# A bank of its own for each feature, two copies ahead of a mask, and stores and loads issued a step later

## The chip, the cores and the metric

The kernel runs on one core of one Trainium2 chip. The metric is the device time of one execution in microseconds. Its engines are TensorE (PE, with its weight loads as PEld), VectorE (DVE), ScalarE (ACT), GpSimd (POOL) and SyncE (SP), which here issues all DMAs from one queue, in order.

## What is computed

Block attention, then two expert layers without routing, all in float32. The matmuls run on pairs of float32r numbers (a high part and a low part), three products for each.

```python
x = attention(q, k, v)              # 8 x 8 heads, 576 tokens in blocks of 64, head size 64
h = x @ moe_w_in                    # 4608 x 512 @ 512 x 2048
g = maximum(h, 0) + alpha * minimum(h, 0)
x = g @ moe_w_out                   # 2048 x 512
h = x @ moe2_w_in
g = h - tanh(h)
out = g @ moe2_w_out                # 4608 x 512
```

## The kernel before

The 4608 tokens are nine blocks of 512, the 2048 hidden columns 16 features of 128. The program has two halves, and the order of its instructions on each engine is the order in which the code is written.

**First half** (`step_one`, 144 steps, one feature of one block each): an up product of 12 matmuls, a leaky ReLU, a split of its result into high and low part, and the down product of an earlier feature. When a block is done, `put_bank` (L583) copies four PSUM banks to `yst`, a tile with three buffers, and stores them to `ysc`. Beside this the attention of later blocks runs (`raw`, `rawn` and `v` are its loads), and 32 pieces of the second layer's weights are converted: `park_load` (L187) loads one as `rw`, two steps later `park_convert` (L198) makes its high part `whi` and its low part in `mr` and, at the end of that step (L224, L225), stores both to DRAM as `wu` and `wd`. `at(step, ...)` (L729) puts such calls into steps. Loads of attention inputs that belong to the next step are issued after those stores.

**Second half** (`layer_two`, L986): 72 pairs of features, q = 0 to 71, eight to each block; p = q mod 8. The up product of a pair is done by Strassen's scheme: seven products p1, p5, p6, p2, p3, p7, p4 of six matmuls each (L1011, 128x256 outputs), into two PSUM banks h0 and h1, one for each feature. Between them stand the down matmuls of earlier features (`downs`, L972, 128x512), 24 to a pair in four gaps of 5, 7, 7 and 5; pair 0 has 4, 5, 5, 0 and pair 1 has 5, 5, 7, 5. In a pair:

- p1 and p5 go into the halves of h1; ScalarE copies the first to h0 (L1045) and the second to `p5`, a part of `ptb` (L1046); p6 waits for these copies.
- after p6 and p2 VectorE adds into h0 (L1017), which p3 waits for; after p7 it adds into h1, which p4 waits for.
- then `act_g` and `tanhshrink` (L539) make g of each feature: ScalarE does sq, th, w and mask (L546 to L549), VectorE four operations and a COPY_PREDICATED that takes th where the mask says so (L550 to L554). ScalarE splits off the high part (L533) and GpSimd the low part (L536) in the next pair.

So ScalarE does eight operations (four for each feature) and then the two copies of the next pair. h0 is complete with p3, h1 with p4.

The banks alternate by pair. Even pairs have the two banks of one tile (`new_banks`, L320, pool `ps_a`, two banks in one buffer); odd pairs have two tiles of a bank each from `ps_h`. The framework derives an instruction's waits from the tiles it touches.

The down weights of layer two come through a ring of four slots (`fetch_down`, L246): each slot is refilled when its feature is done. Slots 2 and 3 are the place of the last feature of the first half; at the end of pair 0 (L1072) the kernel issues their first loads (`wd_2`, `wd_3`) and one of `wu`. Pair 1 issues the load of the next `yraw` (L612) and, as the last block of the first half is finished in its gaps, four `ysc` stores.

Of the kernel before, what the change touches and what calls it, by code (L numbers as in the profile page):

```python
# [27 lines left out]
def kernel(  # L28
# [19 lines left out]
    nc = tc.nc  # L48
# [17 lines left out]
    att = ctx.enter_context(tc.tile_pool(name="att", bufs=1))  # L66
# [2 lines left out]
    dram = ctx.enter_context(tc.tile_pool(name="dram", bufs=1, space=bass.MemoryType.DRAM))  # L69
    ps_h = ctx.enter_context(tc.tile_pool(name="ps_h", bufs=2, space=bass.MemoryType.PSUM))  # L70
    ps_y = ctx.enter_context(tc.tile_pool(name="ps_y", bufs=1, space=bass.MemoryType.PSUM))
    ps_a = ctx.enter_context(tc.tile_pool(name="ps_a", bufs=1, space=bass.MemoryType.PSUM))

    ident = const.tile([P, P], F32, name="ident")
    nalpha_sb = const.tile([P, KF], F32, name="nalpha_sb")
# [2 lines left out]
    edge_sb = const.tile([P, 1], F32, name="edge_sb")  # L78
    xar = xpool.tile([P, 2, 2, KD, NB], F32R, name="xar")
# [7 lines left out]
    wsplit = {}  # L87
# [103 lines left out]
    wu2, wd2, park_raw = {}, {}, {}  # L191
# [11 lines left out]
    def park_convert(kind, n, c):  # L203


        mr = wide.tile([P, 8, P], F32, tag="r", name="mr", bufs=1)
        flat = mr.rearrange("p s m -> p (s m)")
        to_f32_b([to_f32_a(park_raw.pop((kind, n, c)), flat[:, :512], flat.bitcast(I32)[:, 512:])])
        hi = wide.tile([P, 8, P], F32R, tag="w", name="whi")
        if kind == "d":  # L210
            m, h, lo = mr[:, 0:4], hi[:, 0:4], mr[:, 4:8]
            wd2[n] = dram.tile([P, 2, 4, P], F32, name=f"wd2_{n}")
            to = [wd2[n][:, i] for i in range(2)]
        else:
            for o, x, y, op in ((4, 1, 3, ALU.add), (1, 0, 1, ALU.subtract), (5, 4, 0, ALU.subtract),
                                (6, 2, 5, ALU.subtract)):
                nc.gpsimd.tensor_tensor(out=mr[:, o], in0=mr[:, x], in1=mr[:, y], op=op)  # L217
            m, h, lo = mr[:, 0:7], hi[:, 0:7], mr[:, 0:7]
            if n not in wu2:
                wu2[n] = dram.tile([P, 7, 2, 2, P], F32, name=f"wu2_{n}")  # L220
            to = [wu2[n][:, :, i, c] for i in range(2)]
        nc.scalar.activation(out=h, in_=m, func=AF.Copy)
        nc.gpsimd.tensor_tensor(out=lo.bitcast(F32R), in0=m, in1=h.bitcast(F32), op=ALU.subtract)
        nc.sync.dma_start(out=to[0], in_=h.bitcast(F32))  # L224
        nc.sync.dma_start(out=to[1], in_=lo)  # L225

    wu_home = {}

    def fetch_up(d):
        wu_home[d] = home(d, [P, 4, 2, 2, P], F32R, "wu")  # L230
        u = 4 * d
        while u < 4 * d + 4:
            n, o = divmod(u, 7)
            k = min(7 - o, 4 * d + 4 - u)
            nc.sync.dma_start(out=wu_home[d][:, u - 4 * d:u - 4 * d + k].bitcast(F32), in_=wu2[n][:, o:o + k])
            u += k
# [78 lines left out]
    def new_banks(name):  # L315

        return ps_a.tile([P, 2, 512], F32, tag="a", name=name)
# [192 lines left out]

    sq2 = None

    def act_g(layer, f, hp, n):
        g = gpool.tile([P, n], F32, tag="g", name="g", bufs=2)
        if layer == 1:
            tanhshrink(g, hp, n, f)
        else:
            neg = stage.tile([P, 512], F32, tag="st", name="neg")[:, :n]
            nc.scalar.activation(out=neg, in_=hp, func=AF.Relu, scale=-1.0)  # L519
            nc.scalar.activation(out=g, in_=hp, func=AF.Relu)  # L520
            nc.vector.scalar_tensor_tensor(  # L521
                out=g, in0=neg, scalar=nalpha_sb[:, f:f + 1], in1=g, op0=ALU.mult, op1=ALU.add
            )
        hi = gpool.tile([P, n], F32R, tag="ghi", name="ghi")
        lo = gpool.tile([P, n], F32R, tag="glo", name="glo")
        return g, hi, lo
# [11 lines left out]
    def tanhshrink(g, hp, n, f):  # L538


        ca, cb, ce, cc = TS
        sq = sq2[:, f % 2]
        w = att.tile([P, n], F32, tag=("p", "pt")[f % 2], name="w")
        th = vpool.tile([P, n], F32, tag="v", name="th")
        mask = ktc.rearrange("p u h c d -> p (u h c d)")[:, f % 2 * n:(f % 2 + 1) * n]
        nc.scalar.activation(out=sq, in_=hp, func=AF.Square)  # L546
        nc.scalar.activation(out=th, in_=hp, func=AF.Tanh)
        nc.scalar.activation(out=w, in_=sq, func=AF.Square, bias=bias_sb)  # L548
        nc.scalar.activation(out=mask, in_=sq, func=AF.Relu, bias=edge_sb)  # L549
        nc.vector.scalar_tensor_tensor(out=g, in0=sq, scalar=cc, in1=hp, op0=ALU.mult, op1=ALU.mult)  # L550
        nc.vector.tensor_tensor(out=th, in0=hp, in1=th, op=ALU.subtract)  # L551
        nc.vector.scalar_tensor_tensor(out=g, in0=w, scalar=ce, in1=g, op0=ALU.add, op1=ALU.mult)  # L552
        nc.vector.scalar_tensor_tensor(out=g, in0=sq, scalar=ca, in1=g, op0=ALU.add, op1=ALU.mult)  # L553
        nc.vector.copy_predicated(g, mask.bitcast(U32), th)  # L554

    def down(layer, f, g, acc, ends, cuts=((0, 4),)):
        w = wsplit[f, 1]
# [109 lines left out]
    def at(step, fn, *args, first=False):  # L667


        place = {att_s: 0, att_v: 0, att_a_natural: 0, att_a: 3, park_convert: 4, convert: 4, split_w: 4}.get(  # L670
            fn, 1 if first else 2)
        events.setdefault(step, ([], [], [], [], []))[place].append((fn, args))
# [312 lines left out]
    def downs(n):  # L985
        for _ in range(min(n, len(todo))):  # L986
            todo.pop(0)()

    def layer_two(queue, late):
# [1 line left out]

        H = NB // 2
        nonlocal sq2
        banks0, sq2 = new_banks("hps"), att.tile([P, 2, NB], F32, tag="qt", name="sq2")
        p5s = ptb.rearrange("p e h a i -> p (e h a i)").rearrange("p (u t) -> p u t", u=2)

        def leave(j):
# [3 lines left out]
        for layer, f, g, acc, j, t0, ends in queue:  # L1001
            todo.extend(down_items(layer, f, g, acc, ends, lambda f=f: wsplit[f, 1], leave(j) if f == ends[1] else None))
        split_g(*late.pop(), nc.vector)
        nc.tensor.matmul(out=banks0[:, 0], lhsT=wsplit[KF - 1, 1][:, 0, 0:P], rhs=xar[:, 0, 0, 0], start=True, stop=True)
        pairs = {0: (banks0[:, 0], banks0[:, 1])}

        def product(name, n, p, o, start=False):
            w, x = w_up(p, name), XSLOT[n, name]
# [19 lines left out]
            todo[-1] = (lambda last: lambda: (last(), release()))(todo[-1])  # L1028

        LATER = (0, 2, 4, 5, 6, 7)  # L1030
        made, accs = [], {}
        for q in range(NPAIR * n1):
            n, p = divmod(q, NPAIR)
            if q == 1:
                pairs[1] = tuple(ps_h.tile([P, NB], F32, tag="h", name="hps") for _ in range(2))
            h0, h1 = pairs[q % 2]
            p5 = p5s[:, q % 2]
            gaps = (5, 7, 7, 5) if q > 1 else (4, 5, 5, 0) if q == 0 else (5, 5, 7, 5)
            if p == 0:
                accs[n] = []  # L1040
            if p == 1 and n + 1 < n1:
                load_y(n1 + n + 1)
            product("p1", n, p, h1[:, :H], start=True)
            product("p5", n, p, h1[:, H:])
            nc.scalar.activation(out=h0[:, :H], in_=h1[:, :H], func=AF.Copy)  # L1045
            nc.scalar.activation(out=p5, in_=h1[:, H:], func=AF.Copy)  # L1046
            downs(gaps[0])
            product("p6", n, p, h1[:, :H])
            product("p2", n, p, h0[:, :H])
            add(h0[:, H:], h1[:, :H], p5)  # L1050
            for op in (x_ops(n)[9:] if p == 0 and n else x_ops(n + 1)[7:9] if p == NPAIR - 1 and n + 1 < n1 else ()):
                op()
            for m in made:
                split_hi(*m[2])
            for m in reversed(made):
                split_lo(*m[2], nc.gpsimd)
            if n + 1 < n1 and 2 <= p < NPAIR - 1:
                for op in x_ops(n + 1)[LATER[p - 2]:LATER[p - 1]]:
                    op()
            downs(gaps[1])  # L1060
            if made:
                enlist(*made[0])
            product("p3", n, p, h0[:, H:])
            product("p7", n, p, h1[:, :H])
            add(h1[:, H:], h1[:, :H], p5)
            downs(gaps[2])
            product("p4", n, p, h1[:, :H])
            downs(gaps[3])
            if made:
                enlist(*made[1])  # L1070
            made = [(n, 2 * p + e, act_g(1, 2 * p + e, hp, NB), accs[n]) for e, hp in enumerate((h0, h1))]
            if q == 0:  # L1072
                ring_slots(KF - 2)
                for i in (2, 3):
                    fetch_down(i)
                fetch_up(KF - 3)
        downs(KF)
        for m in made:
            split_g(*m[2], nc.vector)
# [41 lines left out]
```

## Time and profile before

| | us |
|---|---|
| median of 3 runs | 1771.32 (1770.65 to 1772.48) |
| the profiled execution | 1773.57 |
| its span | 1771.8 |
| TensorE busy | 1652.6 (93%) |
| VectorE busy | 1167.4 (66%) |
| ScalarE busy | 980.7 (55%) |
| GpSimd busy | 412.8 (23%) |

The span is that of the profiled execution alone, 1.8 us less than its whole time. TensorE is the busiest engine and has about half of the chain that ended last (51%); its busy time is near the span, so what can be won is the time in which it waits. The first half ends at about 890 us. All stretches, starts and waits in the rows are microseconds from the start of the span.

### The profile page before, as it was taken

Reading aid. Unit: us, or ns where it says so; the run is one execution under the profiler, and the core shown is the slowest. Engines: PE = TensorE matmul, PEld = TensorE weight load, DVE = VectorE, ACT = ScalarE, POOL = GpSimd, SP = SyncE. Lnnn points to the kernel's source line nnn. Section 1 sums busy time; section 2 is a strip of 40 time slices with the busy share of each in tenths; the row PEclk is TensorE's granted clock in tenths of the full one; section 3 lists DMA queues with packets and bytes.
Section 4 is the critical chain, followed back from the end, with each engine's and each line's share of the span. In section 5 each row is a group of like instructions: output and inputs, shape, how many; then the busy total and the mean of one; then the engine's idle time right before and its main releaser. Section 6 shows DMA issues by size and latency. Waiting matters only on the chain.

```text
span 1771.8 us, 28197 instructions
## 1 busy us (share of the span) xinstructions
PE 1652.6 (93%) x10702; PEld 1397.4 (79%) x10702; DVE 1167.4 (66%) x1829; ACT 980.7 (55%) x1796; POOL 412.8 (23%) x348
## 2 busy tenths in 40 slices
PE   7899999999998999999979898989898998989898
PEld 6688888888887888788867787877777787878777
DVE  7878756775775767654236666676666666666666
ACT  5666544554554554544336556556565656565554
POOL 1000001111121111112104334342333333333321
PEclk9999999999999999999989999999999999999999
DMA  9551524443544444426632333323242424243232
GB/s 244 166 172 34 130 63 105 113 120 105 129 104 114 104 135 96 133 63 211 214 131 94 119 97 111 117 92 132 87 141 84 143 87 132 91 132 95 90 113 83
DMA packets 259383, 209.47 MB, mean 118 GB/s; under 512 B 173216, under 2 KB 210096, under 8 KB 258224
## 3 DMA queue, kind: packets, MB, share of 16 engines
q1 hardware_dynamic: 259248, 207.68, 39.5%
q8 instruction: 84, 1.38, 0.3%
q14 instruction: 51, 0.42, 0.1%
HBM read 163.59 MB, written 44.04 MB: 117 GB/s over the span
## 4 chain that ended last, share of the span: by engine, by line
PE 51%; DVE 9%; ACT 5%; issue 4%; DMA 2%; POOL 2%; SPq 1%; DVEq 0%; POOLq 0%; ACTq 0%
PE y L972 17%; PE hps L1011 15%; PE y L563 9%; PE hps L505 9%; DVE g L550 2%; DVE g L553 2%; DVE g L552 2%; SPq L308 1%; DVE th L551 1%; DMA ysc<-yst 1%; ACT w L548 1%; ACT ktc L549 1%; ACT sq L546 1%; POOL glo L536 1%; DVE hps L1017 1%
## 5 line engine op out<-in xcount | busy, mean ns | idle before, releaser
L505 PE MATMUL hps<-xar,w 128*128 128x512 f32 (+1 forms) x1740 | 422.2, 392 | 5.9 <-ACT kt L342 5.3
L505 PEld LDWEIGHTS hps<-xar,w 128*128 128x128 f32 x1740 | 328.7, 190 | 74.9 <-ACT kt L342 5.8
L1011 PEld LDWEIGHTS hps<-xar,wu 128*128 128x128 f32 x2160 | 286.4, 191 | 84.1 <-ACT ptb L1046 53.9
L1011 PE MATMUL hps<-xar,wu 128*128 128x256 f32 x2160 | 303.6, 285 | 51.7 <-ACT ptb L1046 42.1
L972 PE MATMUL y<-wd,ghi 128*128 128x512 f32 x1152 | 321.3, 394 | 8.7 <-ACT yst L588 8.7
L533 ACT ACTIVATE ghi<-g 128x512 fp32r<-128x512 f32 x288 | 181.5, 630 | 247.9 <-DVE g L554 143.5
L563 PE MATMUL y<-ghi,w 128*128 128x512 f32 x1136 | 296.9, 394 | 6.4 <-ACT yst L588 5.0
L536 POOL TENSOR_TENSOR glo<-g,ghi 128x512 fp32r<-128x512 f32 x142 | 180.8, 1294 | 495.1 <-ACT ghi L533 252.8
L563 PEld LDWEIGHTS y<-ghi,w 128*128 128x128 f32 x1136 | 210.2, 188 | 51.8 <-ACT yst L588 5.5
L972 PEld LDWEIGHTS y<-wd,ghi 128*128 128x128 f32 x1152 | 203.9, 190 | 37.6 <-ACT yst L588 9.1
L546 ACT ACTIVATE sq<-hps 128x512 f32<-128x512 f32 x144 | 86.3, 600 | 194.9 <-PE hps L1011 188.1
L521 DVE SCALAR_TENSOR_TENSOR g<-neg,nalpha_sb,g 128x512 f32<-128x512 f32 x144 | 107.9, 749 | 122.8 <-ACT g L520 122.8
L536 DVE TENSOR_TENSOR glo<-g,ghi 128x512 fp32r<-128x512 f32 x146 | 131.3, 899 | 82.6 <-ACT ghi L533 82.1
L550 DVE SCALAR_TENSOR_TENSOR g<-sq,hps 128x512 f32<-128x512 f32 x144 | 98.2, 682 | 128.7 <-PE y L972 107.4
L972 PE MATMUL y<-wd,glo 128*128 128x512 f32 x576 | 166.1, 395 | 5.8 <-POOL glo L536 5.8
L1017 DVE TENSOR_TENSOR hps<-hps,ptb 128x256 f32<-128x256 f32 x144 | 62.5, 434 | 155.5 <-PE hps L1011 155.3
L563 PE MATMUL y<-glo,w 128*128 128x512 f32 x568 | 162.6, 390 | 0.2
L519 ACT ACTIVATE neg<-hps 128x512 f32<-128x512 f32 x144 | 85.6, 594 | 125.2 <-PE hps L505 123.3
L1011 PE MATMUL hps<-xw,wu 128*128 128x256 f32 x864 | 126.2, 285 | 23.6 <-ACT ptb L1046 20.5
L1011 PEld LDWEIGHTS hps<-xw,wu 128*128 128x128 f32 x864 | 116.3, 191 | 36.6 <-ACT ptb L1046 25.9
L217 POOL TENSOR_TENSOR mr<-mr 128x128 f32<-128x128 f32 x64 | 33.9, 540 | 473.5 <-DVE mr L138 471.0
L554 DVE COPY_PREDICATED g<-ktc,th 128x512 f32<-128x512 uint32 x144 | 123.3, 856 | 15.5 <-DVE g L553 0.5
(113 smaller groups left out, 2031.0 us busy)
## 6 DMA issues: line engine op xcount, KB each, us to landing
wd<-wd SPq DMA_DIRECT2D x144, 512.0 KB, 3.5
yraw<-ysc SPq DMA_DIRECT2D x9, 1024.0 KB, 6.1
out_dram<-yst SPq DMA_DIRECT2D x36, 256.0 KB, 2.2
raww<-in_moe_w_in_dram SPq DMA_DIRECT2D x16, 512.0 KB, 5.6
v<-in_v_dram SPq DMA_DIRECT2D x32, 256.0 KB, 3.9
raww<-in_moe_w_out_dram SPq DMA_DIRECT2D x16, 512.0 KB, 5.6
rw<-in_moe_w_in_dram SPq DMA_DIRECT2D x16, 512.0 KB, 4.7
rw<-in_moe_w_out_dram SPq DMA_DIRECT2D x16, 512.0 KB, 4.4
```

Source lines behind the costliest of these rows:

```text
L505: nc.tensor.matmul(out=hp[:, cols], lhsT=w[:, a, m], rhs=x[b][:, kk, cols], start=(kk == 0 and i == 0), stop=(kk == KD - 1 and i == 2),)
L519: nc.scalar.activation(out=neg, in_=hp, func=AF.Relu, scale=-1.0)
L521: nc.vector.scalar_tensor_tensor(out=g, in0=neg, scalar=nalpha_sb[:, f:f + 1], in1=g, op0=ALU.mult, op1=ALU.add)
L533: nc.scalar.activation(out=hi, in_=g, func=AF.Copy)
L536: lo_engine.tensor_tensor(out=lo, in0=g, in1=hi.bitcast(F32), op=ALU.subtract)
L546: nc.scalar.activation(out=sq, in_=hp, func=AF.Square)
L550: nc.vector.scalar_tensor_tensor(out=g, in0=sq, scalar=cc, in1=hp, op0=ALU.mult, op1=ALU.mult)
L554: nc.vector.copy_predicated(g, mask.bitcast(U32), th)
L563: nc.tensor.matmul(out=acc[t], lhsT=lhsT, rhs=rhs, start=(f == ends[0] and i == 0), stop=(f == ends[1] and i == 2))
L972: nc.tensor.matmul(out=acc[t], lhsT=lhsT, rhs=rhs, start=(f == ends[0] and i == 0), stop=(f == ends[1] and i == 2))
L1011: nc.tensor.matmul(out=o, lhsT=w[:, a, c], rhs=x[:, b, c], start=start and i == 0 and c == 0, stop=i == 2 and c == 1, skip_group_check=True,)
L1017: nc.vector.tensor_tensor(out=o, in0=a, in1=b, op=ALU.add)
```

## The change

1. **Banks.** `ps_a` is closed when the second half begins, and a pool `ps_b` of single banks takes its place: an even pair's h0 and h1 are two tiles (`hpb`).
2. **Mask.** `tanhshrink` returns its last two instructions, mask and COPY_PREDICATED, as a function `end`. For the first feature of a pair it is called at once, as before. For the second it is called in the next pair, behind the copies L1045 and L1046.
3. **Ring.** The first loads of slots 2 and 3 and that of `wu` are issued at the end of pair 1, not of pair 0.
4. **Stores.** `park_convert` no longer stores; `park_store` does so in the step behind it, after that step's attention loads and ahead of the next `park_load`.

```diff
-        nc.sync.dma_start(out=to[0], in_=h.bitcast(F32))
-        nc.sync.dma_start(out=to[1], in_=lo)
+        park_raw[kind, n, c] = ((to[0], h.bitcast(F32)), (to[1], lo))
+
+    def park_store(kind, n, c):
+        for to, x in park_raw.pop((kind, n, c)):
+            nc.sync.dma_start(out=to, in_=x)
...
-        nc.scalar.activation(out=mask, in_=sq, func=AF.Relu, bias=edge_sb)
+
+        def end():
+            nc.scalar.activation(out=mask, in_=sq, func=AF.Relu, bias=edge_sb)
+            nc.vector.copy_predicated(g, mask.bitcast(U32), th)
+
...
-        nc.vector.copy_predicated(g, mask.bitcast(U32), th)
+        return end
...
     for i, park in enumerate(parks):
+        if i:
+            at(2 * KF + 4 + 3 * i, park_store, *parks[i - 1])
         at(2 * KF + 4 + 3 * i, park_load, *park)
         at(2 * KF + 6 + 3 * i, park_convert, *park)
+    at(2 * KF + 4 + 3 * len(parks), park_store, *parks[-1])
...
-        banks0, sq2 = new_banks("hps"), att.tile([P, 2, NB], F32, tag="qt", name="sq2")
+        pairs_ctx.close()
+        ps_b = ctx.enter_context(tc.tile_pool(name="ps_b", bufs=2, space=bass.MemoryType.PSUM))
+        banks0 = [ps_b.tile([P, NB], F32, tag="b", name="hpb") for _ in range(2)]
+        sq2 = att.tile([P, 2, NB], F32, tag="qt", name="sq2")
...
             nc.scalar.activation(out=p5, in_=h1[:, H:], func=AF.Copy)
+            while ends:
+                ends.pop()()
             downs(gaps[0])
...
-            made = [(n, 2 * p + e, act_g(1, 2 * p + e, hp, NB), accs[n]) for e, hp in enumerate((h0, h1))]
-            if q == 0:
+            made = [(n, 2 * p + e, act_g(1, 2 * p + e, hp, NB, ends if e else None), accs[n]) for e, hp in enumerate((h0, h1))]
+            if q == 1:
                 ring_slots(KF - 2)
```

No instruction is added or taken away on TensorE, VectorE, ScalarE or GpSimd. Three places show what moves. What stands in brackets are the counters that an instruction waits for: those of engines, or of DMAs (DMAHW).

ScalarE, from the end of pair 2 (even) to the copies of pair 3; ktc is the mask. Before:

```order
L546 ACTIVATE sq_8761<-hps 128x512 [waits DVE_49,PE_49]
L547 ACTIVATE th<-hps 128x512
L548 ACTIVATE w<-sq_8761,bias_sb 128x512 [waits Activation_49]
L549 ACTIVATE ktc<-sq_8761,edge_sb 128x512
L546 ACTIVATE sq_8761<-hps 128x512 [waits DVE_49]
L547 ACTIVATE th<-hps 128x512
L548 ACTIVATE w<-sq_8761,bias_sb 128x512 [waits Activation_49]
L549 ACTIVATE ktc<-sq_8761,edge_sb 128x512
L1045 ACTIVATE hps<-hps 128x256 [waits PE_49]
L1046 ACTIVATE ptb<-hps 128x256
```

And now:

```order
L554 ACTIVATE sq_8766<-hpb 128x512 [waits PE_49]
L555 ACTIVATE th<-hpb 128x512
L556 ACTIVATE w<-sq_8766,bias_sb 128x512 [waits Activation_49]
L559 ACTIVATE ktc<-sq_8766,edge_sb 128x512
L554 ACTIVATE sq_8766<-hpb 128x512 [waits DVE_49,PE_49]
L555 ACTIVATE th<-hpb 128x512
L556 ACTIVATE w<-sq_8766,bias_sb 128x512 [waits Activation_49]
L1063 ACTIVATE hps<-hps 128x256 [waits PE_49]
L1064 ACTIVATE ptb<-hps 128x256
L559 ACTIVATE ktc<-sq_8766,edge_sb 128x512
```

The mask of the second feature went from before the two copies to behind them, and the first sq lost its wait for VectorE; the second sq has one for TensorE. In the programs the counter that the first sq waits for stands at p4's last matmul before, and at p3's last matmul now; in odd pairs it stands at p3's in both.

SP, pairs 0 to 2; wd_2 and wd_3 are the first loads of ring slots 2 and 3. Before:

```order
L235 DMA wu<-wu_7_7888 128x1536 [waits DMAHW2_49]
L250 DMA wd<-wd_2_3995 128x1024 [waits DMAHW3_49,PE_49]
L250 DMA wd<-wd_3_4142 128x1024 [waits DMAHW4_49]
L235 DMA wu<-wu_7_7888 128x2048 [waits DMAHW5_49]
L612 DMA yraw<-ysc_2616 128x4x512 [waits DMAHW6_49,Pool_49]
L589 DMA ysc_8762<-yst 128x512 [waits DMAHW7_49,Activation_49]
L589 DMA ysc_8762<-yst 128x512 [waits DMAHW0_49,Activation_49]
L589 DMA ysc_8762<-yst 128x512 [waits DMAHW1_49,Activation_49]
L589 DMA ysc_8762<-yst 128x512 [waits DMAHW2_49,Activation_49]
L250 DMA wd<-wd_4_4716 128x1024 [waits DMAHW3_49,PE_49]
```

And now:

```order
L239 DMA wu<-wu_7_7888 128x1536 [waits DMAHW2_49]
L624 DMA yraw<-ysc_2616 128x4x512 [waits DMAHW3_49,Pool_49]
L601 DMA ysc_8767<-yst 128x512 [waits DMAHW4_49,Activation_49]
L601 DMA ysc_8767<-yst 128x512 [waits DMAHW5_49,Activation_49]
L601 DMA ysc_8767<-yst 128x512 [waits DMAHW6_49,Activation_49]
L601 DMA ysc_8767<-yst 128x512 [waits DMAHW7_49,Activation_49]
L254 DMA wd<-wd_4_4716 128x1024 [waits DMAHW0_49,PE_49]
L254 DMA wd<-wd_2_3995 128x1024 [waits DMAHW1_49]
L254 DMA wd<-wd_3_4142 128x1024 [waits DMAHW2_49]
L239 DMA wu<-wu_7_7888 128x2048 [waits DMAHW3_49]
```

The load of yraw and the four stores of ysc stand ahead of wd_2 and wd_3 now; wd_4, the refill of slot 0, stands ahead of these too and waits for the end of pair 1.

SP in the first half, where one block of tokens ends (at about 530 us of the trace). Before:

```order
L106 DMA rw<-in_moe_w_out_dram 128x512
L308 DMA raw<-in_q_dram 32x8x32 x7
L224 DMA wd_6_5417<-whi 128x512
L225 DMA wd_6_5417<-mr 128x512
L308 DMA raw<-in_q_dram 32x8x32 x7
L269 DMA v<-in_v_dram 128x8x64
L106 DMA rw<-in_moe_w_out_dram 128x512
L589 DMA ysc_5474<-yst 128x512 x4
```

And now:

```order
L107 DMA rw<-in_moe_w_out_dram 128x512
L312 DMA raw<-in_q_dram 32x8x32 x14
L273 DMA v<-in_v_dram 128x8x64
L229 DMA wd_6_5417<-whi 128x512
L229 DMA wd_6_5417<-mr 128x512
L107 DMA rw<-in_moe_w_out_dram 128x512
L601 DMA ysc_5474<-yst 128x512 x4
```

The two stores of converted weights (whi and mr) stand behind 14 attention loads, not between 7 and 7.

## Rows read from the trace of the kernel before

**Rows 1.** Busy time by stretch: length, PE, PEld, DVE, ACT, POOL, granted clock, DMA

```profile
100.00:300.00 200.00, 200.00 (x1324) 163.94 (x1323) 145.55 (x227) 109.02 (x183) 5.86 (x8) 1.00 0.35 87
900.00:1000.00 100.00, 81.62 (x480) 70.58 (x479) 61.38 (x94) 55.20 (x105) 30.72 (x24) 0.95 0.34 111
1200.00:1400.00 200.00, 179.27 (x1095) 156.13 (x1094) 132.87 (x203) 120.91 (x230) 73.92 (x56) 1.00 0.36 118
```

**Rows 2.** TensorE's waits: total us, times, longest

```profile
PE hps L1011 <- ACT ptb L1046: 62.6, 36, 2.8
PE hps L1011 <- DVE hps L1017: 11.9, 9, 1.5
PE y L972 <- ACT yst L588: 8.7, 1, 8.7
PE y L972 <- POOL glo L536: 5.8, 8, 0.7
```

**Rows 3.** Timeline of pairs 26 to 28: start, length, instruction, idle before

```profile
1211.62 1.60 PE L1011 MATMUL hps<-xar,wu 128*128 128x256 f32 x12
...
1213.65 0.39 ACT L1046 ACTIVATE ptb<-hps 128x256 f32<-128x256 f32 x1
...
1214.22 1.59 PE L1011 MATMUL hps<-xar,wu 128*128 128x256 f32 x12
...
1214.54 0.77 DVE L554 COPY_PREDICATED g<-ktc,th 128x512 f32<-128x512 uint32 x1
...
1215.92 0.43 DVE L1017 TENSOR_TENSOR hps<-hps,ptb 128x256 f32<-128x256 f32 x1 [0.60 <-PE hps L1011]
...
1217.26 0.88 PE L1011 MATMUL hps<-xar,wu 128*128 128x256 f32 x6
...
1220.31 0.88 PE L1011 MATMUL hps<-xw,wu 128*128 128x256 f32 x6
...
1221.22 0.60 ACT L546 ACTIVATE sq<-hps 128x512 f32<-128x512 f32 x1 [4.14 <-PE hps L1011]
...
1222.18 1.59 PE L1011 MATMUL hps<-xar,wu 128*128 128x256 f32 x12
...
1225.30 0.72 ACT L549 ACTIVATE ktc<-sq,edge_sb 128x512 f32<-128x512 f32 x1
...
1226.65 1.70 PE L1011 MATMUL hps<-xar,wu 128*128 128x256 f32 x12 [1.71 <-ACT ptb L1046]
...
1234.72 1.48 PE L1011 MATMUL hps<-xar,wu 128*128 128x256 f32 x11
```

**Rows 4.** Timeline of pair 31, VectorE beside GpSimd

```profile
1273.81 1.57 POOL L646 TENSOR_TENSOR xar<-yraw,xar 128x512 fp32r<-128x512 f32 x1 [6.38 <-ACT xar L645]
...
1274.26 1.67 DVE L553 SCALAR_TENSOR_TENSOR g<-sq,g 128x512 f32<-128x512 f32 x1
```

**Rows 5.** Timeline of pairs 0 to 2, where the second half begins

```profile
890.62 1.60 PE L1011 MATMUL hps<-xar,wu 128*128 128x256 f32 x12
...
899.28 0.60 ACT L546 ACTIVATE sq<-hps 128x512 f32<-128x512 f32 x1 [6.24 <-PE hps L1011]
...
910.90 11.33 SPq L589 DMA_DIRECT2D ysc<-yst  x4
...
921.29 0.60 ACT L588 ACTIVATE yst<-y 128x512 f32<-128x512 f32 x1 [12.39 <-DMA ysc<-yst]
...
923.39 2.47 PE L1011 MATMUL hps<-xar,wu 128*128 128x256 f32 x12
```

**Rows 6.** Timeline: the last pair's first product

```profile
1746.10 1.60 PE L1011 MATMUL hps<-xar,wu 128*128 128x256 f32 x12
```

**Rows 7.** Timeline of the first half, one block of tokens ends

```profile
528.41 3.43 SPq L308 DMA_DIRECT2D raw<-in_q_dram  x7
...
533.05 5.91 SPq L589 DMA_DIRECT2D ysc<-yst  x4
...
538.02 0.60 ACT L588 ACTIVATE yst<-y 128x512 f32<-128x512 f32 x1 [7.40 <-DMA ysc<-yst]
```

More of the change, by code (lines that the diff above doesn't have):

```diff
@@ L71 @@
     ps_y = ctx.enter_context(tc.tile_pool(name="ps_y", bufs=1, space=bass.MemoryType.PSUM))
-    ps_a = ctx.enter_context(tc.tile_pool(name="ps_a", bufs=1, space=bass.MemoryType.PSUM))
+    pairs_ctx = ctx.enter_context(ExitStack())
+    ps_a = pairs_ctx.enter_context(tc.tile_pool(name="ps_a", bufs=1, space=bass.MemoryType.PSUM))
     ident = const.tile([P, P], F32, name="ident")
@@ L511, with act_g @@
     sq2 = None
-    def act_g(layer, f, hp, n):
+    def act_g(layer, f, hp, n, ends=None):
         g = gpool.tile([P, n], F32, tag="g", name="g", bufs=2)
         if layer == 1:
-            tanhshrink(g, hp, n, f)
+            end = tanhshrink(g, hp, n, f)
+            if ends is None:
+                end()
+            else:
+                ends.append(end)
         else:
@@ L1003, in layer_two @@
         split_g(*late.pop(), nc.vector)
-        nc.tensor.matmul(out=banks0[:, 0], lhsT=wsplit[KF - 1, 1][:, 0, 0:P], rhs=xar[:, 0, 0, 0], start=True, stop=True)
-        pairs = {0: (banks0[:, 0], banks0[:, 1])}
+        nc.tensor.matmul(out=banks0[0], lhsT=wsplit[KF - 1, 1][:, 0, 0:P], rhs=xar[:, 0, 0, 0], start=True, stop=True)
+        pairs = {0: tuple(banks0)}
         def product(name, n, p, o, start=False):
@@ L1030, in layer_two @@
         LATER = (0, 2, 4, 5, 6, 7)
-        made, accs = [], {}
+        made, accs, ends = [], {}, []
         for q in range(NPAIR * n1):
@@ L1076, in layer_two @@
                 fetch_up(KF - 3)
+        ends.pop()()
         downs(KF)
```

## The prediction

> **What bounds the kernel now.** I read the busy time by stretch first. In the first half TensorE is busy without a gap (200.00 of 200 us), at the full granted clock of 1.00, which is 2.4 GHz. In the second half it is busy 179.27 of 200 us at the same clock, and 81.62 of 100 us at a mean of 0.95 where that half begins [rows 1]. No other engine is above 133 of 200 there. So the second half is TensorE's work plus TensorE's waits, and the list of its waits says which: 62.6 us in 36 waits for ACT's copy L1046, 11.9 us for VectorE's add L1017, one wait of 8.7 us for the copy yst, 5.8 us for glo [rows 2]. The timeline then shows where the 62.6 us come from. In pair 26, an even one, p3 starts at 1217.26 and p4 at 1220.31; ScalarE has idled 4.14 us when its first sq starts at 1221.22, just as p4 ends (1220.31 + 0.88), although h0 has been complete since p3. Its eight operations and two copies then run to 1226.6, and pair 27's p6 starts at 1226.65 after a wait of 1.71 us. Behind pair 27, an odd one, there is none: in pair 26 the copy L1046 begins at 1213.65, ends at 1214.04, and p6 starts at 1214.22 with no idle time noted [rows 3]. The wait list of the first sq has TensorE's p4 in even pairs and p3 in odd ones, as the section on the change says; both features of an even pair stand in one tile.
>
> **The price of an even pair's late start.** Pair 26 takes 10.56 us from its p1 to the next (1211.62 to 1222.18) and holds no wait of TensorE. Pair 27 does the same number of matmuls in 12.54 us (1222.18 to 1234.72) [rows 3]. The loss is 1.98 us, a little more than the 1.71 us shown as idle. Pair 26 is therefore my measure of a pair without a wait, and everything above 10.56 us in the second half is the stock that the change can draw on.
>
> **Banks (part 1).** Even pairs get the waits that odd pairs have. What follows an odd pair is an even one, so a pair such as 26 is an image of what each pair becomes. Pairs 2 to 70 run from 923.39 [rows 5] to 1746.10 [rows 6], 822.71 us for 69 pairs; at 10.56 us each they are 728.6 us. The difference of 94.1 us is more than 34 late odd pairs times 1.98 us (67.3 us). The rest is what comes after the late start in the same pairs: VectorE's chain of the second feature, late by the same time, runs into GpSimd's work (pair 31: GpSimd's L646 of 1.57 us at 1273.81, and an L553 of 1.67 us beside it [rows 4], where a COPY_PREDICATED of the same 128x512 took 0.77 in pair 26 [rows 3]), and the add is late for p3, or glo for the first down product of a block; those are the 11.9 and 5.8 us [rows 2]. With the chain starting earlier these fall away too. The slack says by how much: in pair 26 VectorE idles 0.60 us before its add at 1215.92, which ends at 1216.35, 0.91 us before p3 [rows 3]; so it may be 1.5 us late for nothing. Two GpSimd operations beside the chain cost it some 0.9 us each (1.67 against 0.77), 1.8 us in a pair with two such, 0.3 us above the slack. I leave 0.4 us in each of eight blocks, 3.2 us (an estimate from those rows), and book **90.9 us**. Pair 71, which is odd, gives **2.0 us** more. The Trainium skill, SBUF — State Buffer, section "SBUF: two separate sides", says that VectorE and GpSimd share a port pair by an exclusive lock, and that the one that starts first has it "for the whole instruction". By that rule two such operations of GpSimd could hold VectorE for 2 x 1.57 us, 1.6 us beyond the slack, so 13 us in eight blocks and not 3.2, and the sum would end near 1671 us; the one collision in the rows, where L553 ends 0.55 us behind L646, agrees with a lock, but cost 0.9 us. The bounds: with pair 71, if each of the 35 late pairs kept 0.4 us more it would be 79 us, if nothing stayed 96 us.
>
> **Mask (part 2).** The mask takes ScalarE 0.72 us [rows 3]. In the image pair 26 the copies wait for p5, not for the mask, so taking it away from before them gives nothing there. What it adds is a wait: COPY_PREDICATED of the second feature now waits for a mask behind copies that wait for p5, and the add that p3 needs stands behind it in VectorE's queue. Worked through in pair 26: copies end at 1214.04, mask by 1214.8, COPY_PREDICATED (0.77 us) by 1215.6, add possible from there; it started at 1215.92 and may start at 1216.8. Cost 0, with 1.2 us of cover; without the cover it would cost the mask's 0.72 us in a pair. Only the split L533 moves back by 0.6 us, and with it glo; at the first pair of a block I see about 0.2 us of cover for that, so 0 to 0.5 us in eight pairs, inside the bounds above.
>
> **Ring (part 3).** At 910.90 SP issues the four ysc stores, behind wd_2, wd_3, a wu and the 1 MB of yraw; the first has landed only when the fourth yst copy starts at 921.29 after 12.39 us of idle time, and TensorE lost 8.7 us of that [rows 2, 5]. Now yraw is issued as soon as SP gets there, and the stores as their yst copies end, ahead of the three loads, so the buffer is free in time. The waiting p6 of pair 1 (2.8 us, the longest of the 36 [rows 2]) goes with part 1, and with the gaps the stretches at half the granted clock (1.2 GHz) behind them, which show in the mean of 0.95 [rows 1]. Pairs 0 and 1 take 32.77 us (890.62 to 923.39) [rows 5]. A down matmul is worth 0.22 us (p6 to p3 is 3.04 us with seven of them, p1 to p6 2.60 us with five [rows 3]), and these two pairs have 12 fewer than 48: 21.12 - 12 x 0.22 = 18.5 us. Something new is late there: pair 0 has no down matmuls behind p4 and pair 1 two fewer ahead of p3, so VectorE's chain has about 2 us less room against 1.5 us of slack, and glo follows it. I leave 2.0 us (estimate; 0 to 4) and book **12.3 us**. What moves behind the stores: wd_2 now also stands behind wd_4, which waits for the end of pair 1, and is needed 7.1 us later (p1 to p4 is 8.69 us, of which the last seven down matmuls are 1.6 us behind the point [rows 3]); two loads of 512 KB fit into that, but with little left. If not, pair 2 waits up to 3 us, inside that bound.
>
> **Stores (part 4).** Where a block ends at 530 us, seven attention loads (3.43 us from 528.41) stand ahead of the ysc stores because the two weight stores held them up. The first ysc store is issued at 533.05, and the fourth yst copy waits until 538.02, with 7.40 us of idle time ahead of it [rows 7]; its PSUM bank is the next that a down product needs. With those loads issued in SP's waiting time the store goes about 3.4 us earlier. I take **5 us**, the 3.4 us and 1.6 us (estimate) for TensorE at half its clock behind the gap, as it is behind that of pair 1; the bounds are 0 and 7. The other 30 pairs of stores move past loads where TensorE has no wait; each has two steps, over 10 us, until its buffer mr is written again.
>
> **Sum.** 90.9 + 2.0 + 12.3 + 5 = 110.2 us. From the profiled execution's 1773.57 us that leaves 1663.4 us. That execution is 2.25 us above the median of the runs, so I predict **1661 us**.
>
> **Rivals.**
> *GpSimd beside VectorE becomes the bound.* With every pair at 10.56 us, GpSimd's eleven extra operations of a block (L646 and L649) fall beside VectorE's chain more often. If the four pairs of a block that have two of them each wait 1.5 us for the add, the longest that TensorE did [rows 2], 4 x 1.5 - 0.4 = 5.6 us stay in each of eight blocks: 45 us, 1706 us. For it: 1.67 against 0.77 us [rows 3, 4]. Against it: the even pairs, which are the image, have the same kinds of operations beside them and took 10.56 us. Chance 0.12.
> *The change does not do what it says, since the tiles are not what holds the first sq.* Then only the mask's 0.72 us leaves the path of the 36 waits (26 us), with 10 us of part 3 and 5 us of part 4: 41 us, 1730 us. Against it stands the idle 4.14 us that ends with p4. Chance 0.04.
> *Slower than before.* The new loop p5, copies, mask, COPY_PREDICATED, add, p3 closes in each pair. It has 1.2 us of cover; to undo 110 us it would have to lose 1.55 us in each of 71 pairs, so be 2.75 us late, which needs a mask of about 3.5 us where it took 0.72. Then the time is 1773 us or more. For it: each link is a wait of another engine in an in-order queue. Against it: the durations above. Chance 0.02.
>
> **Numbers.** Forecast 0.80; GpSimd 0.12; tiles 0.04; slower 0.02; still lower, 0.02. With every bound at its best the gain is 96 + 14.3 + 7 = 117 us (1654 us), with every one at its worst 79 + 10.3 + 0 = 89 us (1682 us); the range, 1652 to 1690 us, is a little wider on the side of the GpSimd rival. No change means within 0.2%, about what measuring this kernel can tell: faster 0.97, same 0.01, slower 0.02.
>
> **What would show it.** TensorE's waits for the copy L1046 (now at another line) shrink from 62.6 us to under 5 us; the first sq of an even pair follows p3; pairs alternate no more between 10.56 and 12.54 us; the fourth yst copy waits under 3 us both at 530 and near 910 us; TensorE is busy over 195 of 200 us between 1100 and 1500 us at a granted clock of 1.00. I am wrong if TensorE's waits for the add or for glo grow by more than 10 us, or if its clock falls in the denser half.

## The result, and the profile after

The changed kernel takes **1672.67 us** (median of 4 runs, 1671.51 to 1673.78), beside 1771.9 us for the kernel before on the same chip: a ratio of 0.944 (95% interval 0.9424 to 0.9457), 99 us less. The prediction was 1661 us with a range of 1652 to 1690 us. The profiled execution took 1671.86 us, its span is 1670.1 us.

Busy time by stretch of the changed kernel; columns as in [rows 1], which are the same stretches of before.

```profile
100.00:300.00 200.00, 200.00 (x1324) 163.94 (x1323) 145.52 (x228) 109.82 (x185) 6.96 (x10) 1.00 0.35 87
900.00:1000.00 100.00, 99.47 (x622) 89.26 (x621) 71.48 (x111) 65.92 (x125) 40.90 (x31) 1.00 0.42 138
1200.00:1400.00 200.00, 198.07 (x1229) 176.56 (x1228) 145.01 (x223) 131.84 (x249) 84.79 (x64) 1.00 0.37 119
```

The first half is as full as it was. The second goes from 179.27 to 198.07 of 200 us, and where it begins from 81.62 to 99.47 of 100 us, at the full granted clock in place of a mean of 0.95. TensorE's waits (engine, tile and line, what it waited for: total us, times, longest), to be read against [rows 2], and below them two of ScalarE's:

```profile
PE hpb L1029 <- DVE hpb L1035: 5.2, 14, 0.5
PE hps L1029 <- DVE hps L1035: 2.3, 8, 0.5
PE hpb L1029 <- ACT ptb L1064: 1.5, 2, 0.8
PE y L575 <- ACT yst L600: 1.4, 1, 1.4
PE y L987 <- POOL glo L544: 0.8, 1, 0.8
ACT yst L600 <- DMA out_dram<-yst: 18.2, 7, 3.6
ACT yst L600 <- DMA ysc<-yst: 12.7, 6, 4.5
```

The 62.6 us for the copy of p5 are 1.5 us. The wait for the fourth yst copy where the second half begins (8.7 us) is gone, the one near 530 us fell from 5.0 to 1.4 us. What is left is the add. ScalarE has a wait of 18.2 us in seven pieces that was absent at these places before: its fourth yst copy waits for an out store to land. Half a microsecond of TensorE here and there looks small (7.5 us in all for the add), but the pairs show more. The table gives the time from the p1 of a pair to the next p1, read from the timeline, as the median over blocks 1 to 7, by the place of the pair in its block:

| kernel | 0 | 1 | 2 | 3 | 4 | 5 | 6 | 7 |
|---|---|---|---|---|---|---|---|---|
| before | 10.56 | 13.55 | 10.56 | 12.55 | 10.95 | 12.55 | 10.56 | 14.26 |
| changed | 10.56 | 10.60 | 11.38 | 11.07 | 11.08 | 10.56 | 10.56 | 10.56 |
| yraw early (e6) | 10.56 | 10.57 | 10.56 | 10.56 | 10.73 | 10.56 | 10.56 | 10.56 |
| yraw late (e7) | 10.56 | 10.57 | 10.56 | 10.56 | 10.73 | 10.56 | 10.56 | 10.56 |
| operations later (e8) | 10.56 | 10.57 | 11.56 | 10.56 | 10.56 | 10.73 | 10.56 | 12.46 |

The alternation of 10.56 and 12.55 is gone. Pairs 2, 3 and 4 of a block are 0.5 to 0.8 us above 10.56 us (in two blocks, 2 and 7, pair 2 is 1.8 above; there the first out store is 5.9 and 5.6 us on its way). In block 0 of the changed kernel these pairs take 10.56 us, though GpSimd's preparing operations are there too; its second pair stores no out, and its four ysc stores come 8 us after its yraw has landed and take 2.0 to 2.4 us. In block 8 they take 10.56 us too; there is neither an operation for a next block nor a load of yraw.

Where the 101.7 us between the two profiled executions went: 8.2 us ahead of the first p1 (890.62 to 882.45; 1.9 of them arise before 95 us, where the change does nothing), 12.5 us in pairs 0 and 1 (32.77 to 20.32), 78.9 us in pairs 2 to 70 (822.71 to 743.77), 2.2 us in pair 71 (25.69 to 23.54).

The changed kernel around pairs 25 and 26 (places 1 and 2 of block 3), SP's queue, then ScalarE, VectorE, TensorE (start, us, engine, line, operation; in brackets the idle time ahead of it and what ended it):

```profile
1151.27 0.52 SPq L624 DMA_DIRECT2D yraw<-ysc  x1
1154.12 5.62 SPq L601 DMA_DIRECT2D out_dram<-yst  x4
...
1153.49 0.60 ACT L600 ACTIVATE yst<-y 128x512 f32<-128x512 f32 x1
1155.37 1.09 ACT L600 ACTIVATE yst<-y 128x512 f32<-128x512 f32 x2
1158.78 0.60 ACT L600 ACTIVATE yst<-y 128x512 f32<-128x512 f32 x1 [2.33 <-DMA out_dram<-yst]
1159.28 0.59 ACT L554 ACTIVATE sq<-hps 128x512 f32<-128x512 f32 x1
...
1160.47 0.69 DVE L562 SCALAR_TENSOR_TENSOR g<-sq,hps 128x512 f32<-128x512 f32 x1 [2.06 <-ACT th L555]
1167.16 0.43 DVE L1035 TENSOR_TENSOR hpb<-hpb,ptb 128x256 f32<-128x256 f32 x1
1171.31 1.11 DVE L564 SCALAR_TENSOR_TENSOR g<-w,g 128x512 f32<-128x512 f32 x1
1172.45 1.67 DVE L565 SCALAR_TENSOR_TENSOR g<-sq,g 128x512 f32<-128x512 f32 x1
...
1167.65 0.97 PE L1029 MATMUL hpb<-xar,wu 128*128 128x256 f32 x6 [0.54 <-DVE hpb L1035]
1178.72 0.97 PE L1029 MATMUL hps<-xar,wu 128*128 128x256 f32 x6 [0.26 <-DVE hps L1035]
```

The chain of waits names the first link, a store that is 4.57 us on its way (start, us, what):

```profile
1153.60 0.50 ACT yst L600
1154.12 4.57 DMA out_dram<-yst
...
1158.78 0.60 ACT yst L600
1159.38 0.49 ACT sq L554
```

There are three yst buffers, so the fourth copy waits for the first store to land. That store is issued 2.85 us behind the 1 MB load of yraw. Behind the fourth copy, in ScalarE's queue, stands the sq of pair 25's first feature, so VectorE's chain starts late (2.06 us idle for th) and ends in an add that is late for pair 26's p3. In pair 26 two of GpSimd's preparing operations lengthen VectorE's operations (1.11 and 1.67 us where others take 0.69), so pair 27's add is late again.

**Theory A:** the landing of the out store starts this, and without it the pairs would be at 10.56 us. **Theory B**, the rival of the prediction: GpSimd beside VectorE does it by itself. The kernel before had the same buffers and no such wait at these places; its yraw was issued 4.36 us ahead of the first store (1198.62 and 1202.98 in block 3), because ScalarE got to the first yst copy of that pair only at 1202.35, late from the pair ahead of it.

### The profile page after: what moved, and what is told of

Same layout as the page of the kernel before. It is cut to its first block, busy times and chain, and to the rows that moved or that the text cites. A ratio compares the mean times of both kernels' runs of the same rounds, so it can differ in the third digit from the quotient of the medians.

```text
span 1670.1 us, 28092 instructions
## 1 busy us (share of the span) xinstructions
PE 1636.7 (98%) x10702; PEld 1396.5 (84%) x10702; DVE 1161.5 (70%) x1829; ACT 978.1 (59%) x1796; POOL 413.5 (25%) x348
## 4 chain that ended last, share of the span: by engine, by line
PE 58%; DVE 6%; ACT 4%; DMA 3%; issue 3%; POOL 0%; SPq 0%; DVEq 0%; ACTq 0%; POOLq 0%
PE y L987 17%; PE y L575 12%; PE hps L509 12%; PE hpb L1029 8%; PE hps L1029 8%; DMA out_dram<-yst 2%; DVE g L565 1%; DVE g L564 1%; DVE g L560 1%; ACT ktc L559 1%; DVE g L562 1%; ACT yst L600 1%; ACT w L556 1%; PE sc L372 1%; ACT sq L554 0%
## 5 line engine op out<-in xcount | busy, mean ns | idle before, releaser
L1029 PEld LDWEIGHTS hpb<-xar,wu 128*128 128x128 f32 x1080 | 143.5, 191 | 17.3 <-DVE hpb L1035 7.9
L1029 PEld LDWEIGHTS hps<-xar,wu 128*128 128x128 f32 x1080 | 144.1, 191 | 12.6 <-DVE hps L1035 4.4
L1029 PE MATMUL hpb<-xar,wu 128*128 128x256 f32 x1080 | 150.3, 284 | 4.4 <-DVE hpb L1035 3.7
L1029 PE MATMUL hps<-xar,wu 128*128 128x256 f32 x1080 | 149.7, 283 | 1.8 <-DVE hps L1035 1.8
L987 PEld LDWEIGHTS y<-wd,glo 128*128 128x128 f32 x576 | 108.4, 188 | 24.3 <-POOL glo L544 2.7
L575 PEld LDWEIGHTS y<-glo,w 128*128 128x128 f32 x568 | 106.5, 188 | 23.2 <-DVE glo L544 1.1
L560 DVE COPY_PREDICATED g<-ktc,th 128x512 f32<-128x512 uint32 x144 | 110.2, 765 | 14.8
L565 DVE SCALAR_TENSOR_TENSOR g<-sq,g 128x512 f32<-128x512 f32 x144 | 114.3, 794 | 5.0
```

Of the source, the lines that this page charges most:

```text
L575: nc.tensor.matmul(out=acc[t], lhsT=lhsT, rhs=rhs, start=(f == ends[0] and i == 0), stop=(f == ends[1] and i == 2))
L987: nc.tensor.matmul(out=acc[t], lhsT=lhsT, rhs=rhs, start=(f == ends[0] and i == 0), stop=(f == ends[1] and i == 2))
L1029: nc.tensor.matmul(out=o, lhsT=w[:, a, c], rhs=x[:, b, c], start=start and i == 0 and c == 0, stop=i == 2 and c == 1, skip_group_check=True,)
```

## The experiments

The kernel before took 1771.25 us beside e1 to e4, 1770.93 us beside e5 to e8 and 1771.0 us beside e9 and e10, so the times are compared as they stand. In brackets behind each time stand its ratio to the kernel before and the 95% interval.

**e1: the banks alone.** The kernel before with

```diff
-        banks0, sq2 = new_banks("hps"), ...
...
+        pairs_ctx.close()
+        ps_b = ctx.enter_context(tc.tile_pool(name="ps_b", bufs=2, space=bass.MemoryType.PSUM))
+        banks0 = [ps_b.tile([P, NB], F32, tag="b", name="hpb") for _ in range(2)]
...
-        pairs = {0: (banks0[:, 0], banks0[:, 1])}
+        pairs = {0: tuple(banks0)}
```

> The kernel before with part 1 alone: each bank of an even pair is a tile of its own; mask, ring loads and weight stores stand as before. If the banks carry the gain and the mask lies under cover, pairs 2 to 71 fall as in the changed kernel (79 + 2 us measured there) and only the two yst waits near 530 and 910 us stay: 1690 us, 1686 to 1694, and no pair in the second half is above 11.5 us except the first two. If instead the mask stood on the path of every pair once the banks are apart, some 0.3 to 0.7 us more in each of 70 pairs: 1710 to 1740 us.

Measured: 1691.1 us (0.9547, 0.9533 to 0.9561), 80 us less than before. TensorE's waits in it:

```profile
PE y L973 <- ACT yst L589: 8.8, 3, 7.3
PE hpb L1015 <- ACT ptb L1050: 5.2, 6, 1.4
PE y L564 <- ACT yst L589: 4.5, 1, 4.5
```

Both yst waits stay, and the 62.6 us for the copy fell to 5.2. Not as expected: six pairs besides the first two are above 11.5 us (11.60 to 12.45), all at places 1 and 2 of a block. One is pair 2, behind the long yst wait; the others show the late start of the section above, which ScalarE's 17.1 us of waits for out stores in this kernel go with.

**e2: everything but the banks.** The changed kernel with the lines of e1 taken back.

> The changed kernel with both banks of an even pair in one tile again; mask behind the copies, ring loads and stores as changed. If the shared tile holds the first sq, TensorE's long waits for the copy of p5 are back in the 35 odd pairs; parts 3 and 4 give 12 + 6 us, and the mask, which here does stand ahead of copies that TensorE waits for, up to 0.7 us in each of 35 pairs: 1730 us if it all counts, 1754 us if none does; the first sq of even pairs is again released by p4. If the tile is not the holder, 1673 us as the changed kernel.

Measured: 1754.97 us (0.9906, 0.9891 to 0.992). ScalarE's and TensorE's waits, then pair 26: its p4, and the sq of its first and its second feature:

```profile
ACT sq L553 <- PE hps L1025: 192.0, 90, 6.3
PE hps L1025 <- ACT ptb L1060: 40.8, 36, 2.2
PE hps L1025 <- DVE hps L1031: 25.4, 44, 2.1
```

```profile
1202.68 0.88 PE L1025 MATMUL hps<-xw,wu 128*128 128x256 f32 x6
...
1203.60 0.60 ACT L553 ACTIVATE sq<-hps 128x512 f32<-128x512 f32 x1 [2.89 <-PE hps L1025]
...
1206.10 0.60 ACT L553 ACTIVATE sq<-hps 128x512 f32<-128x512 f32 x1 [0.19 <-DVE th L562]
```

The first sq starts as p4 ends (1202.68 + 0.88) again, and pairs 2 to 70 take 822.64 us, against 822.71 before. The shared tile holds the first sq; the rival that it doesn't falls. The mask does leave the path of the waiting copy, and the wait for it falls from 62.6 to 40.8 us; but the add's wait grows from 11.9 to 25.4 us, and an odd pair goes only from 12.55 to 12.41. The 16 us that are left are the ring and the stores.

**e3: the mask where it was.** The changed kernel with

```diff
-            while ends:
-                ends.pop()()
...
-            act_g(1, 2 * p + e, hp, NB, ends if e else None)
+            act_g(1, 2 * p + e, hp, NB)
...
-        ends.pop()()
```

> The changed kernel with the second feature's mask and its COPY_PREDICATED where they were, ahead of the two copies. By my prediction the mask is worth nothing once the banks are apart: 1672 us, 1669 to 1675. Rival: it delays the copies of p5 by up to 0.72 us in each pair and TensorE waits for them: 1690 to 1720 us, with waits for the copy of p5 in most pairs. Second rival: the wait that the moved mask adds costs something now, and the time falls by 2 to 6 us.

Measured: 1673.68 us (0.9446, 0.9432 to 0.9461), the same as the changed kernel. The wait for the copy of p5 is 5.2 us here (1.5 with the mask behind), those for the add 3.5 us (7.5): it moves a little from one to the other.

**e4: the ring loads behind pair 0 again.** One line of the changed kernel.

```diff
-            if q == 1:
+            if q == 0:
                 ring_slots(KF - 2)
```

> The changed kernel with the ring loads issued behind pair 0 again. My term was 12.3 us for pairs 0 and 1, of which 8.7 us are the wait for the fourth yst copy; 2.8 us of the 12.3 were the first wait for the copy of p5, which goes with the banks and not with the ring. So 8 to 11 us longer than the changed kernel: 1680 to 1684 us, the fourth yst copy idle over 10 us again near 905 us, and the granted clock below 1.00 behind it. If the order of the loads is not what holds the store, 1672 us.

Measured: 1681.58 us (0.9491, 0.9475 to 0.9507), 8.9 us more than the changed kernel. SP, ScalarE and TensorE where the second half begins, then the busy time of that stretch:

```profile
897.58 0.38 SPq L624 DMA_DIRECT2D yraw<-ysc  x1
898.08 11.41 SPq L601 DMA_DIRECT2D ysc<-yst  x4
...
908.54 0.60 ACT L600 ACTIVATE yst<-y 128x512 f32<-128x512 f32 x1 [11.07 <-DMA ysc<-yst]
...
909.19 1.22 PE L987 MATMUL y<-wd,ghi 128*128 128x512 f32 x2 [6.95 <-ACT yst L600]
```

```profile
880.00:930.00 50.00, 41.74 (x246) 36.43 (x245) 24.92 (x39) 24.66 (x48) 9.13 (x7) 0.90 0.38 127
```

The long wait is back, and the granted clock falls to a mean of 0.90. In the changed kernel this stretch has 48.69 of 50 us at 1.00; SP issues the four stores from 894.38, and the last two yst copies run at 896.88 without a wait.

**e5: both stores issued by the conversion.** The changed kernel with

```diff
-        park_raw[kind, n, c] = ((to[0], h.bitcast(F32)), (to[1], lo))
+        nc.sync.dma_start(out=to[0], in_=h.bitcast(F32))
+        nc.sync.dma_start(out=to[1], in_=lo)
...
-        if i:
-            at(2 * KF + 4 + 3 * i, park_store, *parks[i - 1])
...
-    at(2 * KF + 4 + 3 * len(parks), park_store, *parks[-1])
```

> The changed kernel with both stores of each converted weight issued by its conversion again. My term was 5 us (0 to 7); the two traces show 6.2 us less from 95 us to the start of the second half. So 1677 to 1679 us, with the fourth yst copy near 533 us idle about 7 us again and TensorE's gap of 5 us behind it. If the two traces differ there for another reason: 1672 us.

Measured: 1677.3 us (0.9475, 0.9461 to 0.9489), 4.6 us more than the changed kernel. The profiled execution is the longest of its four, 1681.5 us. Its SP queue, its fourth yst copy and TensorE's wait for that, then the queue and the copy of the changed kernel:

```profile
526.69 3.44 SPq L309 DMA_DIRECT2D raw<-in_q_dram  x7
...
531.34 6.85 SPq L598 DMA_DIRECT2D ysc<-yst  x4
...
537.25 0.60 ACT L597 ACTIVATE yst<-y 128x512 f32<-128x512 f32 x1 [8.39 <-DMA ysc<-yst]
...
PE y L572 <- ACT yst L597: 6.2, 1, 6.2
```

```profile
527.29 6.06 SPq L601 DMA_DIRECT2D ysc<-yst  x4
533.40 0.97 SPq L312 DMA_DIRECT2D raw<-in_q_dram  x2
...
532.41 0.60 ACT L600 ACTIVATE yst<-y 128x512 f32<-128x512 f32 x1 [4.49 <-DMA ysc<-yst]
```

The seven loads stand ahead of the ysc stores again, as in [rows 7], and the copy waits 3.9 us longer; TensorE's wait behind it is 6.2 us, where the changed kernel has 1.4 and the kernel before 5.0.

**e6 and e7: the load of yraw away from the out stores.** The changed kernel with the load ahead of two ring loads in pair 0 of a block (e6), or right behind the fourth out store (e7):

```diff
 e6
-            if p == 1 and n + 1 < n1:
+            if q == 1 and n + 1 < n1:
                 load_y(n1 + n + 1)
...
+            if p == 0 and n and n + 1 < n1:
+                load_y(n1 + n + 1)
             for m in made:
                 split_hi(*m[2])
 e7, with the first line as in e6, in write_out
                 put_bank(a, out[...], ...)
+                if t == 3 and n + 2 < n1:
+                    load_y(n1 + n + 2)
```

> The changed kernel with the 1 MB load of yraw issued in the first pair of a block, ahead of two ring loads, and not in the second, 2.9 us ahead of the first out store. My theory on the 12 us that are missing: in the blocks 1 to 7 the fourth yst copy waits for the landing of the first out store (4.6 us, behind yraw on the DMA engines), ScalarE starts the next sq 2.3 us late, and the add of the following three pairs is late by what that leaves. Then that wait is gone, the third, fourth and fifth pair of a block are back at 10.56 to 10.7 us, and the time falls by 10 to 15 us: 1658 to 1663 us. Rival: GpSimd's operations beside VectorE's chain alone make the add late: the pairs stay at 11.3, 11.1 and 11.1 us, 1672 us.

> The changed kernel with the load of yraw issued right behind the four out stores, and not ahead of them. If the store is late because yraw is on the DMA engines ahead of it, it lands in about 2.2 us, and ScalarE's wait is gone as with the early load; but yraw then lands some 8 us later, about 1 us ahead of the next block's first operations on it, so 1658 to 1667 us. If what holds the store is not yraw (the ring loads, or the store itself), 1672 us or more.

Measured: e6 1658.58 us (0.9365, 0.9351 to 0.9379), **e7 1657.91 us (0.9361, 0.9345 to 0.9376)**. Both intervals lie below that of the changed kernel. SP and ScalarE of e7 at the same two pairs, then the busy time of its stretch:

```profile
1149.06 3.43 SPq L601 DMA_DIRECT2D out_dram<-yst  x4
1152.59 0.40 SPq L624 DMA_DIRECT2D yraw<-ysc  x1
...
1150.33 1.81 ACT L600 ACTIVATE yst<-y 128x512 f32<-128x512 f32 x3
1152.20 0.60 ACT L554 ACTIVATE sq<-hps 128x512 f32<-128x512 f32 x1
```

```profile
1200.00:1400.00 200.00, 200.00 (x1248) 179.83 (x1248) 145.77 (x228) 134.87 (x254) 85.42 (x65) 1.00 0.37 122
```

The copies run through, the next sq follows, and TensorE is busy 200.00 of 200 us. The first store goes out 3.4 us behind the pair's p1 in both kernels (1145.65 to 1149.06 here, 1150.70 to 1154.12 in the changed kernel), behind the same ring load, and is 2.0 us on its way in place of 4.57. The median landing of an out store, by the page's list of DMAs (KB each, us to landing), in the changed kernel and in e7:

```profile
out_dram<-yst SPq DMA_DIRECT2D x36, 256.0 KB, 3.3
```

```profile
out_dram<-yst SPq DMA_DIRECT2D x36, 256.0 KB, 2.1
```

Theory A holds: moving one transfer, forward or back, takes 14 to 15 us away, and pairs 2 to 4 are at 10.56, 10.56 and 10.73 us with the same GpSimd operations beside them. By themselves these cost 0.2 us in a block (the median; 0.4 in block 7). In pairs 2 to 70, 730.15 us are left in e7, 1.5 us above 69 times 10.56.

**e8: GpSimd's operations moved on by a pair.** The changed kernel with

```diff
-        LATER = (0, 2, 4, 5, 6, 7)
+        LATER = (0, 0, 2, 4, 5, 7)
```

> The changed kernel with the eleven operations that prepare the next block moved on by one pair: none in the third pair of a block (it had two), then two, two, one, two. If ScalarE's wait for the out store is the cause, the third pair keeps its wait of 0.5 us and its 11.3 us, since they come before GpSimd's first operation there, but VectorE catches up in it, and the fourth and fifth pair fall to 10.56 us: 4 to 7 us less, 1666 to 1669 us. If GpSimd beside VectorE is the cause by itself, the waits move with the operations: 11.1 to 11.3 us in the fourth to seventh pair, 10.6 in the third, 1670 to 1675 us.

Measured: 1681.47 us (0.95, 0.9482 to 0.9517), 8.8 us more than the changed kernel; neither expectation was met as a whole. Places 2 to 4 do as theory A said: 11.56 at place 2, where none of these operations stands, then 10.56 and 10.56 with two each. The late start alone costs about 1 us (the median; up to 1.9), and VectorE catches up in the pair in which nothing is beside it. In the changed kernel, where GpSimd's operations meet the late start, places 2 to 4 lose 1.85 us together (the medians). But the pair at place 7 now takes 12.46 us. VectorE and GpSimd in pair 30 and 31, and TensorE's wait:

```profile
1224.05 1.67 DVE L565 SCALAR_TENSOR_TENSOR g<-sq,g 128x512 f32<-128x512 f32 x1
1228.39 1.67 DVE L565 SCALAR_TENSOR_TENSOR g<-sq,g 128x512 f32<-128x512 f32 x1
1230.16 1.61 DVE L560 COPY_PREDICATED g<-ktc,th 128x512 f32<-128x512 uint32 x1
...
1228.21 1.29 POOL L658 TENSOR_TENSOR xar<-yraw,xar 128x512 fp32r<-128x512 f32 x1 [3.04 <-ACT xar L657]
1229.59 1.60 POOL L661 TENSOR_TENSOR yraw<-yraw 128x512 f32<-128x512 f32 x1
```

```profile
PE hps L1029 <- DVE hps L1035: 13.6, 9, 1.6
```

Two operations at place 6 and two at place 7 fall into one round of VectorE, from one add of p6 to the next. They lengthen its operations by 0.98, 0.98, 0.85 and 0.2 us, 3.0 us together, against a slack of 1.5 us; the wait is 1.63 us. So theory B's price is real, but it is 1.9 us only where four such operations meet in a round; two cost 0 to 0.2 us (places 3 and 4 of e7), three 0.3 us (place 7 of e10, below).

**e9 and e10: what is left in e7.** e9 is e7 with the mask as in e3; e10 is e7 with `LATER = (0, 1, 3, 4, 6, 7)`.

> The changed kernel with yraw behind the out stores (1657.9 us) and the second feature's mask ahead of the two copies again, as before the change. With no late start left, the cover that I named for the mask is whole, so the mask's place should be worth nothing: 1656 to 1660 us. If the mask ahead of the copies holds TensorE where the chain has two of GpSimd's operations beside it, up to 0.7 us in some 14 pairs come back: 1664 to 1668 us. If instead the moved mask is what makes the add of the fifth pair late (10.73 in place of 10.56 us), those pairs fall to 10.56 and the time by 1 us.

> The changed kernel with yraw behind the out stores, and GpSimd's eleven preparing operations spread as one, two, one, two, one in the third to seventh pair of a block, not two, two, one, one, one; the two in the eighth stay. What is left in pairs 2 to 70 is 0.2 us in the fifth pair of seven blocks, behind two subtractions in the fourth. If a pair takes two such operations within its slack, as the third pair does, no more than 1.5 us can be gained or lost: 1656 to 1660 us. If a pair with two of them next to one with one is over the slack, as in the eighth pair of the run with the operations moved on (12.46 us), 1 to 2 us in some of 8 blocks: 1666 to 1674 us.

Measured: e9 1658.65 us (0.9367, 0.9352 to 0.9383) and e10 1659.44 us (0.9369, 0.9355 to 0.9383), neither to be told from e7. In e10 the 0.17 us at place 4 are gone and 0.3 us at place 7 have come. The mask's place is worth nothing here either, and the fifth pair keeps its wait in e9 (10.76 us in the median), so the moved mask is not what makes it late.

## Why the prediction was right, and where it was 12 us off

- **What bounds the second half**: right. The shared tile held the first sq (e2), and with banks of their own the pairs stop alternating. The banks alone bring 80 of the 99 us.
- **Banks, 90.9 us for pairs 2 to 70**: mis-sized. The traces show 78.9 us. The step that failed is "I leave 0.4 us in each of eight blocks, 3.2 us"; 15.1 us stayed (743.77 less 69 times 10.56). It was worked out from the slack in pair 26, a pair in which nothing else is late, and took GpSimd's operations as the only thing to come. The image was wrong at the places 1 to 4 of a block: with the pair starting earlier, the out store is issued 2.85 us behind yraw and not 4.36, ScalarE waits for it, and that uses up the slack that was to cover GpSimd's operations. e6 and e7 take the store's delay away and leave 1.5 to 2.3 us, less than my 3.2: two of GpSimd's operations lengthened VectorE's chain by 1.4 us in pair 26 (1.11 and 1.67 us for two times 0.69), where I had 1.8. I had looked at what stands behind stores in the ring and the first half, and not at the stores of every block. The bound of 79 us for the banks with pair 71 was just wide enough (81.1 measured). One sentence against the GpSimd rival was wrong besides: the even pairs had not all taken 10.56 us; at place 4 they took 10.95.
- **Pair 71, 2.0 us**: 2.15 measured.
- **Mask, 0**: right. e3 and e9 are 1.0 and 0.7 us from the kernels that they are to be compared with, inside the intervals.
- **Ring, 12.3 us**: right, 12.45 in the traces and 20.32 us for pairs 0 and 1 where I had 20.5. Two short new waits (0.5 us for the add, 0.8 for glo) are the late chain that I had left 2 us for. e4 gives 8.9 us for the ring alone.
- **Stores, 5 us**: right within what can be measured; 4.6 by e5. No half-clock stretch stands behind the gap of 1.4 us.
- **GpSimd as the bound, 1706 us**: it did not come; e8 shows where it would, with four operations in one round. From the section "SBUF: two separate sides" of the Trainium skill's page SBUF — State Buffer I had worked out 13 us in eight blocks and a sum near 1671 us, which is where the time came out. That agreement is by chance: with the store out of the way the same operations cost 0.2 us in a block. The rows of e8 do agree with its exclusive lock: L565 ends 0.56 us behind GpSimd's L658 (1230.06 and 1229.50), L560 0.58 us behind its L661 (1231.77 and 1231.19).
- **The signs**: the waits for the copy are under 5 us, the alternation is gone, and TensorE is busy 198 of 200 us at a clock of 1.00, as said. The first sq of pair 26 starts at 1168.94, 1.85 us ahead of p4 (1170.79), where it had followed p4's end. The fourth yst copy doesn't wait near 895 us, but 4.5 us near 530 us, where I had said under 3. The waits for the add and for glo fell, from 11.9 to 7.5 and from 5.8 to 0.8 us; my sign of being wrong, that they grow by 10 us, could not show the 15.1 us that stayed, of which the list notes only about half as waits.

The sum by parts: e1 gives 80.2, the ring 8.9, the stores 4.6, the mask 0 to 1, so 94 to 95 of the 99 us. The rest, 4 to 5 us, was not separated. In e1 pairs 2 to 70 take 749.07 us, 5.3 more than with all parts; 1.8 of these are pair 2, which takes 12.37 us behind the long yst wait, but e4 has that pair too (12.27 us), so it is counted in the ring's 8.9. How late the store lands differs from one execution to another: the same pairs take 746.02 us in the profile of e3 and 746.14 us in that of e5, whose edit ends with the first half, 2.3 us more than the changed kernel's 743.77. So chance may explain much of the rest; that the parts help each other is not shown.

## What to carry to other kernels

A pair without waits is a good image of what all pairs become only if nothing in the loop hangs on the time between two pairs: when a loop gets faster, work out again, for each place in it, how far every transfer is from the one issued ahead of it. Slack that covers one late thing doesn't cover two: look for the places where two users of the same slack meet, since their prices do not simply add: here the late start alone cost about 1 us in a block (e8), GpSimd's operations alone 0.2 us (e7), and both together 1.85 us. And before an operation is moved off a crowded place, count what the round at the new place already holds.

## What the runs showed of the hardware

A 256 KB store from the same queue, issued 2.85 us behind a 1 MB load, was 4.57 us on its way; with the load behind it, the median of the out stores was 2.1 us. That load was itself 6.7 us on its way from 1151.27, so the store landed about 0.7 us behind it (1158.7 against 1158.0), as if it had stood behind it. The Trainium skill, DMA: Bandwidth & Descriptors, section "Queues, rings and completion order", says that each DMA engine consumes the descriptors of a ring in order, which agrees.

A VectorE operation of 128x512 with GpSimd beside it took up to 1.67 us where it takes 0.69, but in e7, which has the same GpSimd operations at the same places as the changed kernel, they cost TensorE 0.2 us in a block, and in e8, where four of them fall into one round, 1.9 us in it.
